# Six kept tiles around the middle layer boundary, and a transfer order in which each layer ends with its last wo block

## The chip, the cores and the metric

The kernel runs on one core of one Trainium2 chip. The metric is device time in microseconds (us), median of repeated runs. "Span" is the length of the one profiled execution; it is about 2 us shorter than the time of the same run.

Engine names as the profile has them: PE is the matmul engine (TensorE), PEld its weight loads, DVE is VectorE, ACT is ScalarE, POOL is GpSimd, SP is SyncE, which here only issues transfers ("SPq" is its queue). L425 is line 425 of the kernel profiled, so line numbers differ between kernels.

## The reference

One decode step of attention for one token, four layers deep. Layers 0 and 2 use the weights and the cache of set A, layers 1 and 3 those of set B. Each set holds K and V of 32 heads, 8192 positions, 192 columns, in bf16.

```python
def block(x, k_cache, v_cache, wq, wo):            # x: 1 x 640
    q = (x @ wq).reshape(32 heads, 192)
    scores = einsum("hd,hkd->hk", q, k) * 192 ** -0.5
    o = einsum("hk,hkd->hd", softmax(scores), v)
    return o.reshape(32 * 192) @ wo

x = x + block(layernorm(x), A_k, A_v, A_wq, A_wo)   # layer 0
x = x + block(layernorm(x), B_k, B_v, B_wq, B_wo)   # layer 1
x = x + block(layernorm(x), A_k, A_v, A_wq, A_wo)   # layer 2: the same cache as layer 0
x = x + block(layernorm(x), B_k, B_v, B_wq, B_wo)   # layer 3: the same cache as layer 1
```

K or V of one head is 8192 x 192 x 2 bytes = 3.146 MB, a "tile" below. Four layers of 64 tiles would be 256 tile loads. A tile that stays on the chip from layer 0 to 2, or from 1 to 3, saves one of them.

## The kernel before

SBUF holds eight slots of one tile each. All transfers go through these slots in one fixed list, `plan`, issued in order by SP; a transfer waits until the work that last read its slot is done. Five V tiles stay in their slot for two layers.

```python
NSLOT = 8
KEPT_A = (3, 9)          # V of these heads of set A stays from layer 0 to layer 2
KEPT_B = (18, 23, 28)    # V of these heads of set B stays from layer 1 to layer 3
...
for l in range(NL):
    for h in range(H):
        if h > 0 and h % HEADS_W == 0 and h <= H - O_LAST:     # before heads 10, 20, 30
            plan.append(("wo", l, h // HEADS_W - 1))           # 2.458 MB, into a slot
            steps.append(("wo", l, h // HEADS_W - 1))
        plan.append(("k", l, h))
        ...                       # m: K * q and its sums, s: softmax, v: p @ V
        plan += [n for n in part if n[0] == "v" and (l < 2 or n[2] not in kept[l % 2])]
        for g in {0: [0], 1: [1, 2]}.get(h, []):               # wq in three parts
            plan.append(("wq", l, g)); steps.append(("wq", l, g))
        if h == H // 2:
            plan.append(("wol", l))                            # last rows of wo, a tile of its own
...
# a slot for each transfer: the one whose holder is released first
i = min(range(NSLOT), key=lambda i: (-1 if holder[i] is None else released(holder[i]), i))
place[n], before[n] = i, holder[i]
```

For one head, DVE multiplies K by q in place in four pieces (L384), PE sums the products (S, L396), the softmax follows, and PE multiplies by V (O, L433). At the end of a layer the outputs of the last two heads are gathered and go through the last rows of wo ("YB" matmuls, L356), and the next layer's q can be computed only then.

Of the kernel before, what the change touches and what calls it, by code (L numbers as in the profile page):

```python
# [59 lines left out]
KEPT_A = (3, 9)  # L60
KEPT_B = (18, 23, 28)


def build(nc, A_x, A_k, A_v, A_wq, A_wo, B_x, B_k, B_v, B_wq, B_wo, out):
# [14 lines left out]
    G = 4  # L79

    with ExitStack() as ctx:
# [12 lines left out]
        wol = sb("wol", [P, OI, D], BF16)  # L94
        orow = sb("orow", [1, HEADS_W * DH], BF16)
        oT = sb("oT", [P, NW], BF16)
        o_sb = sb("o_sb", [P, 2 * DH], F32)
# [67 lines left out]
        kept = {0: KEPT_A, 1: KEPT_B}  # L165
        steps, plan = [], []
        for l in range(NL):
            if l == 0:
                plan.append(("wq0", 0))
            for h in range(H):  # L170
                if h > 0 and h % HEADS_W == 0 and h <= H - O_LAST:
                    plan.append(("wo", l, h // HEADS_W - 1))
                    steps.append(("wo", l, h // HEADS_W - 1))
                plan.append(("k", l, h))
                if h < H - 2:
                    part = [("m", l, h), ("s", l, h), ("v", l, h)]
                elif h == H - 2:
                    part = [("m", l, h)]
                else:
                    part = [("m", l, h), ("s", l, h - 1), ("s", l, h), ("v", l, h - 1), ("v", l, h)]  # L180
                steps += part
                plan += [n for n in part if n[0] == "v" and (l < 2 or n[2] not in kept[l % 2])]
                for g in {0: [0], 1: [1, 2]}.get(h, []):
                    plan.append(("wq", l, g))
                    steps.append(("wq", l, g))
                if h == H // 2:
                    plan.append(("wol", l))
                if h == H // 2 + 4 and l + 1 < NL:
                    plan.append(("wq0", l + 1))
        at = {n: i for i, n in enumerate(steps)}  # L190

        def released(n):

            if n[0] == "v" and n[1] < 2 and n[2] in kept[n[1]]:
                return at[("v", n[1] + 2, n[2])]
            return at[("m",) + n[1:] if n[0] == "k" else n]
# [12 lines left out]
        def transfer(n):  # L209
            l = n[1]  # L210
            w = W[l % 2]
            if n[0] == "wq0":
                return SP.op(lambda s: s.dma_start(
                    wq0[:], w["wq"][:, 0:Q_FIRST * DH].rearrange("(p c) n -> p c n", c=DC)),
                    freed.get(("wq0", l - 1)), sem=semQ0, inc=16)
            if n[0] == "wol":
                return SP.op(lambda s: s.dma_start(
                    wol[:], w["wo"][(H - O_LAST) * DH:H * DH].rearrange("(p i) n -> p i n", p=P)),
                    freed.get(("wol", l - 1)), sem=semOL, inc=16)
            i = place[n]  # L220
            t = slot[i]
            if n[0] in "kv":
                f = lambda s: s.dma_start(t[:], w[n[0]][0, n[2]].rearrange("(p j) d -> p (j d)", p=P))
            elif n[0] == "wq":
# [3 lines left out]
                    w["wq"][:, Q_FIRST * DH:].rearrange("(p c) n -> p c n", c=DC)[:, c0:c0 + k, :])  # L228
            else:
                r0 = n[2] * HEADS_W * DH  # L230
# [13 lines left out]
        def ahead():  # L244

            while issued[0] < len(plan):
# [4 lines left out]
                if m[0] in ("wq0", "wol") and m[1] > 0 and (m[0], m[1] - 1) not in freed:  # L251
                    return
# [7 lines left out]
        for k in "MX QB QT TT TO YB orow oT qT qbc xb rs st stt row_written".split():  # L260
            last[k] = None

        ev_x = SP.op(lambda s: s.dma_start(x_bf[:], A_x[0, 0].rearrange("(p c) -> p c", c=DC)), sem=semX, inc=16)
# [17 lines left out]
        def layer(l, ev_z, ev_true):  # L281
# [68 lines left out]
            def project(n, t3, k):  # L350

                PE.wait(last["oTw"], need(n), last["YB"])
# [213 lines left out]
```

## Time and profile before

2021.47 us, median of 3 runs (2019.82 to 2023.39); the profiled execution has a span of 2016.5 us.

From the page of the kernel before: busy time by engine; rows of the span in 40 slices of 50 us; the transfer totals and queues.

```profile
PE 1408.8 (70%) x10438; PEld 617.4 (31%) x10438; DVE 1047.1 (52%) x1073; ACT 217.1 (11%) x657; POOL 4.6 (0%) x22
GB/s 403 430 430 430 430 429 426 430 430 429 425 432 430 429 428 430 427 430 430 407 401 415 431 428 429 430 426 430 429 429 426 431 430 430 430 429 429 430 429 292
DMA packets 44211, 854.00 MB, mean 424 GB/s; under 512 B 4816, under 2 KB 7376, under 8 KB 7888
q1 hardware_dynamic: 44112, 852.51, 99.0%
q8 instruction: 82, 1.34, 0.3%
q14 instruction: 17, 0.14, 0.0%
```

No engine is near its limit, while the transfers run at 425 to 432 GB/s in nearly every slice. So the transfer stream is the bound, and a tile costs 3.146 MB / 430.5 GB/s = 7.3 us of it (430.5 is the plateau by the landings explained below: undisturbed tiles land 7.306 us apart). The stream is off this plateau at the start, around slices 20 to 22 (the boundary between layers 1 and 2), and at the end. q8 and q14 fetch the program's own instructions.

The end of the kernel, from its chain of waits (start us, length us, what; "x4" merges four instructions):

```profile
1949.65 41.19 DMA slot<-in_B_k_cache_dram
1990.87 6.78 DVE slot L384 x4
1997.69 1.47 PE S L396 x6
...
2003.10 2.35 PE O L433 x32
...
2007.55 2.69 PE O L433 x17
...
2012.37 0.78 PE YB L356 x15
```

The last K lands at 1990.9 us, 25.6 us of dependent work follow, and meanwhile the V tiles of the last two heads still arrive.

A transfer has landed when the last of the 16 DMA engines has raised its semaphore. I read each landing off the semaphore events in the trace. Three columns: the landing on the quickest engine, on the slowest, and how late it is (the gap to the previous landing on the slowest engine, less bytes / 430.5 GB/s). The trace does not name the engine of a landing, so "quickest" and "slowest" may be different engines from one transfer to the next. Kernel before, at the middle boundary:

```
transfer                quickest   slowest    late
K  layer 1, head 31      1004.9     1007.4     0.0
V  layer 1, head 31      1019.6     1022.0     0.0
K  layer 2, head 0       1026.9     1030.5     1.2
wq layer 2, part 0       1041.1     1044.7     0.0
K  layer 2, head 1       1052.7     1054.3     2.2
wq layer 2, part 2       1070.4     1072.4     0.5
K  layer 2, head 2       1078.4     1081.3     1.6
```

### The profile page before, as it was taken

How to read it: one execution, taken by the hardware profiler on the slowest of the kernel's cores; microseconds unless marked ns; L12 is line 12 of the kernel's file. 1: busy time of each engine (PE TensorE's matmuls, PEld its weight loads, DVE VectorE, ACT ScalarE, POOL GpSimd, SP SyncE). 2: the span in 40 equal slices, each digit the busy share in tenths (PEclk: the TensorE clock that was granted, in tenths of full speed). 3: DMA queues.
4: the chain of work that ended last, by engine and by line, in shares of the span. 5: the costliest groups of instructions: out<-in, count | busy, mean ns of one | idle time of the engine just before them, and what ended most of it. 6: DMA issues, size and time to landing. Idle time of an engine off the chain costs nothing.

```text
span 2016.5 us, 23357 instructions
## 1 busy us (share of the span) xinstructions
PE 1408.8 (70%) x10438; PEld 617.4 (31%) x10438; DVE 1047.1 (52%) x1073; ACT 217.1 (11%) x657; POOL 4.6 (0%) x22
## 2 busy tenths in 40 slices
PE   5667666667666766766766777667676667767777
PEld 2223223223332322322333233232233323223323
DVE  3455544555445455456544656546554454655554
ACT  0111111011011111111100111110100111011111
POOL 0000000000000000000000000000000000000000
PEclk8887988888777788788878978888877788888888
DMA  9999999999999999999999999999999999999996
GB/s 403 430 430 430 430 429 426 430 430 429 425 432 430 429 428 430 427 430 430 407 401 415 431 428 429 430 426 430 429 429 426 431 430 430 430 429 429 430 429 292
DMA packets 44211, 854.00 MB, mean 424 GB/s; under 512 B 4816, under 2 KB 7376, under 8 KB 7888
## 3 DMA queue, kind: packets, MB, share of 16 engines
q1 hardware_dynamic: 44112, 852.51, 99.0%
q8 instruction: 82, 1.34, 0.3%
q14 instruction: 17, 0.14, 0.0%
HBM read 852.49 MB, written 0.00 MB: 423 GB/s over the span
## 4 chain that ended last, share of the span: by engine, by line
DMA 68%; PE 17%; DVE 12%; ACT 1%; issue 1%; another core or an unknown queue 0%; SPq 0%; DVEq 0%
DMA slot<-in_B_k_cache_dram 34%; DMA slot<-in_A_k_cache_dram 31%; DVE slot L384 10%; PE S L396 10%; PE O L433 3%; DMA slot<-in_A_wq_dram 3%; PE TB L448 1%; DVE s_sb L403 1%; PE YB L356 1%; ACT p_sb L413 1%; PE TB L417 1%; DVE small L410 0%; PE QM L407 0%; DVE m_bf L406 0%
## 5 line engine op out<-in xcount | busy, mean ns | idle before, releaser
L384 DVE TENSOR_TENSOR slot<-slot,q_sb 128x3072 bf16<-128x3072 bf16 x512 | 865.7, 1753 | 492.1 <-DMA slot<-in_A_k_cache_dram 253.8
L396 PE MATMUL S<-slot,ident 128*128 128x512 bf16 x3072 | 849.4, 434 | 300.0 <-DVE slot L384 299.8
L396 PEld LDWEIGHTS S<-slot,ident 128*128 128x128 bf16 x3072 | 310.4, 109 | 834.6 <-DVE slot L384 442.4
L433 PE MATMUL O<-slot,p_sb 128*2 128x384 bf16 x4096 | 344.3, 417 | 0.0
L403 DVE TENSOR_REDUCE s_sb<-S 128x64 f32<-128x512 f32 x128 | 88.4, 690 | 251.0 <-PE S L396 251.0
L433 PEld LDWEIGHTS O<-slot,p_sb 128*2 128x2 bf16 x4096 | 128.0, 87 | 132.4 <-issue 96.1
L448 PE MATMUL TB<-o_sb,small 128*1 128x192 f32 x480 | 121.6, 386 | 36.5 <-DVE small L421 28.2
L346 ACT ACTIVATE q_sb<-QM 128x192 bf16<-128x192 f32 x120 | 39.6, 330 | 967.6 <-PE QM L339 967.6
L417 PE MATMUL TB<-small,ones 128*128 128x1 f32 x256 | 49.7, 263 | 109.6 <-ACT p_sb L413 109.6
L407 PE MATMUL QM<-ident,m_bf 128*128 128x128 bf16 x128 | 27.7, 217 | 130.8 <-DVE m_bf L406 130.8
L441 ACT ACTIVATE o_sb<-O,small 128x384 f32<-128x384 f32 x128 | 74.3, 580 | 227.2 <-PE O L433 227.2
L421 DVE RECIPROCAL small<-TB 128x1 f32<-128x1 f32 x128 | 21.6, 168 | 122.0 <-PE TB L417 122.0
L413 ACT ACTIVATE p_sb<-s_sb,small 128x64 bf16<-128x64 f32 x128 | 44.5, 348 | 337.5 <-DVE small L410 337.5
L417 PEld LDWEIGHTS TB<-small,ones 128*128 128x128 f32 x256 | 38.8, 191 | 129.4 <-ACT p_sb L413 129.4
L410 DVE TENSOR_REDUCE small<-QM 128x1 f32<-128x128 f32 x128 | 37.3, 291 | 52.3 <-PE QM L407 52.3
L454 ACT ACTIVATE orow<-TB 1x192 bf16<-1x192 f32 x120 | 38.3, 319 | 202.6 <-PE TB L448 202.6
L407 PEld LDWEIGHTS QM<-ident,m_bf 128*128 128x128 bf16 x128 | 12.2, 96 | 148.5 <-ACT q_sb L346 130.5
L448 PEld LDWEIGHTS TB<-o_sb,small 128*1 128x1 f32 x480 | 33.2, 88 | 76.3 <-DVE small L421 37.4
L356 PE MATMUL YB<-oT,slot 128*128 128x1 bf16 x900 | 37.9, 178 | 3.3 <-ACT oT L370 3.3
L356 PEld LDWEIGHTS YB<-oT,slot 128*128 128x128 bf16 x900 | 36.9, 131 | 4.3 <-ACT oT L370 4.3
L339 PEld LDWEIGHTS QM<-ident,qT 128*128 128x128 bf16 x240 | 22.9, 98 | 30.3 <-issue 2.0
L339 PE MATMUL QM<-ident,qT 128*128 128x128 bf16 x240 | 30.3, 209 | 1.6 <-ACT qT L328 1.6
(46 smaller groups left out, 189.3 us busy)
## 6 DMA issues: line engine op xcount, KB each, us to landing
slot<-in_A_k_cache_dram SPq DMA_DIRECT2D x64, 3072.0 KB, 31.6
slot<-in_B_k_cache_dram SPq DMA_DIRECT2D x64, 3072.0 KB, 31.4
slot<-in_A_v_cache_dram SPq DMA_DIRECT2D x62, 3072.0 KB, 32.0
slot<-in_B_v_cache_dram SPq DMA_DIRECT2D x61, 3072.0 KB, 30.5
slot<-in_A_wo_dram SPq DMA_DIRECT2D x6, 2400.0 KB, 30.1
slot<-in_B_wo_dram SPq DMA_DIRECT2D x6, 2400.0 KB, 30.9
slot<-in_A_wq_dram SPq DMA_DIRECT2D x4, 2880.0 KB, 21.2
slot<-in_B_wq_dram SPq DMA_DIRECT2D x4, 2880.0 KB, 31.3
```

The costliest lines, as they stand in the source:

```text
L339: e = PE.op(lambda t, b=b, o=o, n=n, d=done: t.matmul(QM[:, d:d + n], lhsT=qT[:, b:b + 1].broadcast_to([P, P]), rhs=ident[:, o:o + n], sta ...
L346: lambda a: a.activation(q_sb[i][:], QM[:, 0:DH], ACT.Copy), e, last["q"][i], bank=use["QM"])
L356: e = PE.op(lambda t, i=i, c=c, f=y_first[0], fin=fin: t.matmul(YB[:, c:c + 1], lhsT=t3[:, i, c:D:DC], rhs=oT[:, i:i + 1], start=f, stop=f ...
L384: e = DV.op(lambda v, d0=d0: v.tensor_tensor(k3[:, :, d0:d0 + QD], k3[:, :, d0:d0 + QD], q_sb[qi][:, d0:d0 + QD].unsqueeze(1).broadcast_to ...
L396: e = PE.op(lambda t, d0=d0, fin=fin: t.matmul(S[:, :], lhsT=ident[:], rhs=k3[:, :, d0:d0 + R], start=(d0 == 0), stop=fin), signal=fin, ba ...
L403: ev_s = DV.op(lambda v: v.tensor_reduce(s_sb[par][:], S[:].rearrange("p (j r) -> p j r", r=R), AX.X, ALU.add), ev_S[h], last["s"][par], b ...
L407: e = PE.op(lambda t: t.matmul(QM[:, C_MX:C_MX + P], lhsT=m_bf[par][:, 0:1].broadcast_to([P, P]), rhs=ident[:], start=True, stop=True), ev ...
L413: ev_p[h] = AC.op(lambda a: a.activation(p_sb[par][:], s_sb[par][:], ACT.Exp, bias=negm[par][:, 0:1], accum_out=l_col[par][:]), ev_n, ev_s ...
L417: e = PE.op(lambda t: t.matmul(TB[:, C_L + par:C_L + par + 1], lhsT=ones[:], rhs=l_col[par][:], start=True, stop=True), ev_p[h], last["L"] ...
L433: e = PE.op(lambda e, g=g, j=j, f=m < G, fin=fin: e.matmul(OB[par][32 * g:32 * g + 2, 0:2 * DH], lhsT=p_sb[par][:, j:j + 2], rhs=t[:, j * ...
L441: lambda a: a.activation(o_sb[:], OB[par][:, 0:2 * DH], ACT.Copy, scale=rl[par][:, 0:1]),
L448: e = PE.op(lambda t, i=i: t.matmul(TB[0:1, C_O:C_O + DH], lhsT=pick[:, i:i + 1], rhs=o_sb[:, i * DH:(i + 1) * DH], start=(i == 0), stop=( ...
```

## The change

Its intent is to load one tile less, to let the bulk of the last wo transfer run under the last heads' work, and to open layer 2 on tiles that are already there. K and V of head 0 of set A stay from layer 0 to 2, and V of heads 28 to 31 of set B from layer 1 to 3. Layer 3 takes its heads in another order, so that heads 30, 31 (first) and 28, 29 (places 8 and 9, counted from 0) meet their kept V early. In every layer the third wo block and the last wo rows now come after the last V and share one slot. A kept K cannot be multiplied in place, so head 0 of layer 0 writes its products into another slot ("t").

```diff
-KEPT_A = (3, 9)
-KEPT_B = (18, 23, 28)
+KEPT = {0: {("k", 0), ("v", 0)}, 1: {("v", 28), ("v", 29), ("v", 30), ("v", 31)}}
...
+    BACKWARD = dict(heads=[H - 2, H - 1] + list(range(H - HEADS_W, H - 2)) + list(range(O_LAST, H - HEADS_W))
+                    + list(range(O_LAST)), ...)
+    ORDER = [FORWARD, FORWARD, FORWARD, BACKWARD]
...
-        wol = sb("wol", [P, OI, D], BF16)
+        oTl = sb("oTl", [P, OI], BF16)
...
             if l == 0:
+                plan.append(("k", 0, 0))
                 plan.append(("wq0", 0))
+            wq_early = l == 2
+            if wq_early:
+                plan += [("wq", l, g) for g in range(len(Q_PARTS))]
...
+                if wq_early and p == 0:
+                    part = [("wq", l, 0), ("m", l, 0), ("wq", l, 1), ("s", l, 0), ("v", l, 0), ("wq", l, 2)]
...
-                if h == H // 2:
-                    plan.append(("wol", l))
...
+            plan.append(("wo", l, 2))
+            steps.append(("wo", l, 2))
+            plan.append(("wol", l))
...
-        ev_x = SP.op(lambda s: s.dma_start(x_bf[:], ...
+        ev_x = AC.op(lambda s: s.dma_start(x_bf[:], ...
...
+            if l + 1 == NL:      # the last add writes bf16 itself; no cast after it
+                return None, DV.op(lambda v: v.tensor_tensor(x_bf[:], x_true[:], YB[:, 0:DC], ALU.add), ...)
```

More of the change, by code (lines that the diff above doesn't have):

```diff
@@ L79, in build @@
     G = 4
+    FORWARD = dict(heads=list(range(H)), q0=0, q1=Q_FIRST * DH, wo=[0, HEADS_W, 2 * HEADS_W], wol=H - O_LAST)
+    BACKWARD = dict(heads=[H - 2, H - 1] + list(range(H - HEADS_W, H - 2)) + list(range(O_LAST, H - HEADS_W))
+                    + list(range(O_LAST)), q0=(H - Q_FIRST) * DH, q1=0,
+                    wo=[H - HEADS_W, O_LAST, O_LAST + HEADS_W], wol=0)
+    ORDER = [FORWARD, FORWARD, FORWARD, BACKWARD]
     with ExitStack() as ctx:
@@ L162, in build, with head, first_load, stays @@
             ev_zero = DV.op(lambda v, b=b: v.memset(b[:], 0.0), bank=use["O0" if b is OB[0] else "O1"])
-        kept = {0: KEPT_A, 1: KEPT_B}
+        def head(l, p):
+            return ORDER[l]["heads"][p]
+        def first_load(kind, l, p):
+            n = (kind, head(l, p))
+            if l >= 2 and n in KEPT[l - 2]:
+                return (kind, l - 2, ORDER[l - 2]["heads"].index(n[1]))
+            return (kind, l, p)
+        def stays(kind, l, p):
+            return l < 2 and (kind, head(l, p)) in KEPT[l]
         steps, plan = [], []
@@ L168, in build @@
             if l == 0:
+                plan.append(("k", 0, 0))
                 plan.append(("wq0", 0))
-            for h in range(H):
-                if h > 0 and h % HEADS_W == 0 and h <= H - O_LAST:
-                    plan.append(("wo", l, h // HEADS_W - 1))
-                    steps.append(("wo", l, h // HEADS_W - 1))
-                plan.append(("k", l, h))
-                if h < H - 2:
-                    part = [("m", l, h), ("s", l, h), ("v", l, h)]
-                elif h == H - 2:
-                    part = [("m", l, h)]
+            wq_early = l == 2
@@ new lines, in build @@
+            if wq_early:
+                plan += [("wq", l, g) for g in range(len(Q_PARTS))]
+            for p in range(H):
+                if p > 0 and p % HEADS_W == 0:
+                    b = p // HEADS_W - 1
+                    steps.append(("wc", l, b))
+                    if p <= H - HEADS_W:
+                        plan.append(("wo", l, b))
+                        steps.append(("wo", l, b))
+                if first_load("k", l, p) == ("k", l, p) and (l, p) != (0, 0):
+                    plan.append(("k", l, p))
+                if stays("k", l, p):
+                    plan.append(("t", l, p))
+                if wq_early and p == 0:
+                    part = [("wq", l, 0), ("m", l, 0), ("wq", l, 1), ("s", l, 0), ("v", l, 0), ("wq", l, 2)]
+                elif p < H - 2:
+                    part = [("m", l, p), ("s", l, p), ("v", l, p)]
+                elif p == H - 2:
+                    part = [("m", l, p)]
@@ L179, in build @@
                 else:
-                    part = [("m", l, h), ("s", l, h - 1), ("s", l, h), ("v", l, h - 1), ("v", l, h)]
+                    part = [("m", l, p), ("s", l, p - 1), ("s", l, p), ("v", l, p - 1), ("v", l, p)]
                 steps += part
-                plan += [n for n in part if n[0] == "v" and (l < 2 or n[2] not in kept[l % 2])]
-                for g in {0: [0], 1: [1, 2]}.get(h, []):
-                    plan.append(("wq", l, g))
-                    steps.append(("wq", l, g))
@@ L186, in build @@
-                if h == H // 2:
-                    plan.append(("wol", l))
-                if h == H // 2 + 4 and l + 1 < NL:
+                plan += [n for n in part if n[0] == "v" and first_load(*n) == n]
+                if not wq_early:
+                    for g in {0: [0], 1: [1, 2]}.get(p, []):
+                        plan.append(("wq", l, g))
+                        steps.append(("wq", l, g))
+                if p == H // 2 + 4 and l + 1 < NL:
                     plan.append(("wq0", l + 1))
+            plan.append(("wo", l, 2))
@@ L190, in build @@
+            steps.append(("wo", l, 2))
+            plan.append(("wol", l))
         at = {n: i for i, n in enumerate(steps)}
         def released(n):
-            if n[0] == "v" and n[1] < 2 and n[2] in kept[n[1]]:
-                return at[("v", n[1] + 2, n[2])]
-            return at[("m",) + n[1:] if n[0] == "k" else n]
+            if n[0] in "kvt":
+                l, p = n[1:]
+                if n[0] != "t" and stays(*n):
+                    l, p = n[1] + 2, ORDER[n[1] + 2]["heads"].index(head(*n[1:]))
+                return at[("v" if n[0] == "v" else "m", l, p)]
@@ L198, in build @@
+            return at[n]
         place, before, holder = {}, {}, [None] * NSLOT
@@ L210, in transfer @@
             l = n[1]
+            o = ORDER[l]
             w = W[l % 2]
@@ L213, in transfer @@
                 return SP.op(lambda s: s.dma_start(
-                    wq0[:], w["wq"][:, 0:Q_FIRST * DH].rearrange("(p c) n -> p c n", c=DC)),
+                    wq0[:], w["wq"][:, o["q0"]:o["q0"] + Q_FIRST * DH].rearrange("(p c) n -> p c n", c=DC)),
                     freed.get(("wq0", l - 1)), sem=semQ0, inc=16)
             if n[0] == "wol":
+                wol = slot[place[("wo", l, 2)]][:, NW * D:(NW + OI) * D].rearrange("p (i n) -> p i n", n=D)
                 return SP.op(lambda s: s.dma_start(
-                    wol[:], w["wo"][(H - O_LAST) * DH:H * DH].rearrange("(p i) n -> p i n", p=P)),
-                    freed.get(("wol", l - 1)), sem=semOL, inc=16)
+                    wol, w["wo"][o["wol"] * DH:(o["wol"] + O_LAST) * DH].rearrange("(p i) n -> p i n", p=P)),
+                    sem=semOL, inc=16)
             i = place[n]
             t = slot[i]
+            if n[0] == "t":
+                b = before[n]
+                return None if b is None else freed[b]
             if n[0] in "kv":
-                f = lambda s: s.dma_start(t[:], w[n[0]][0, n[2]].rearrange("(p j) d -> p (j d)", p=P))
+                f = lambda s: s.dma_start(t[:], w[n[0]][0, head(*n[1:])].rearrange("(p j) d -> p (j d)", p=P))
             elif n[0] == "wq":
@@ L227, in transfer @@
                     t[:, 0:k * QC].rearrange("p (c n) -> p c n", c=k),
-                    w["wq"][:, Q_FIRST * DH:].rearrange("(p c) n -> p c n", c=DC)[:, c0:c0 + k, :])
+                    w["wq"][:, o["q1"]:o["q1"] + QC].rearrange("(p c) n -> p c n", c=DC)[:, c0:c0 + k, :])
             else:
-                r0 = n[2] * HEADS_W * DH
+                r0 = o["wo"][n[2]] * DH
                 f = lambda s: s.dma_start(
@@ L250, in ahead @@
                     return
-                if m[0] in ("wq0", "wol") and m[1] > 0 and (m[0], m[1] - 1) not in freed:
+                if m[0] == "wq0" and m[1] > 0 and (m[0], m[1] - 1) not in freed:
                     return
@@ L259, in build @@
                     osb=None, orowb=None)
-        for k in "MX QB QT TT TO YB orow oT qT qbc xb rs st stt row_written".split():
+        for k in "MX QB QT TT TO YB orow oT oTl qT qbc xb rs st stt row_written".split():
             last[k] = None
-        ev_x = SP.op(lambda s: s.dma_start(x_bf[:], A_x[0, 0].rearrange("(p c) -> p c", c=DC)), sem=semX, inc=16)
+        ev_x = AC.op(lambda s: s.dma_start(x_bf[:], A_x[0, 0].rearrange("(p c) -> p c", c=DC)), sem=semX, inc=16)
         ahead()
@@ L348, in layer, with project @@
             y_first = [True]
-            def project(n, t3, k):
-                PE.wait(last["oTw"], need(n), last["YB"])
+            def project(n, t3, k, o, ev_o):
+                PE.wait(ev_o, need(n), last["YB"])
                 for i in range(k):
@@ L356, in project @@
                         e = PE.op(lambda t, i=i, c=c, f=y_first[0], fin=fin: t.matmul(
-                            YB[:, c:c + 1], lhsT=t3[:, i, c:D:DC], rhs=oT[:, i:i + 1], start=f, stop=fin,
+                            YB[:, c:c + 1], lhsT=t3[:, i, c:D:DC], rhs=o[:, i:i + 1], start=f, stop=fin,
                             skip_group_check=True), signal=(i == k - 1 and c == DC - 1), bank=use["YB"])
                         y_first[0] = False
-                last["oT"] = freed[n] = e
+                if n != ("wo", l, 2):
+                    freed[n] = e
                 return e
@@ L369, in columns @@
                 last["orow"] = e
-                last["TT"] = last["oTw"] = AC.op(lambda a: a.activation(oT[:, 0:k], TB[:, 0:k], ACT.Copy),
-                                                 e, last["oT"], bank=use["TB"])
+                last["TT"] = AC.op(lambda a: a.activation(oT[:, 0:k], TB[:, 0:k], ACT.Copy),
+                                   e, last["oT"], bank=use["TB"])
             ev_S, ev_p, ev_rl, ev_os = {}, {}, {}, {}
@@ L376, in products @@
                 par = (l * H + h) % 2
-                nk = ("k", l, h)
-                k3 = slot[place[nk]][:].rearrange("p (j d) -> p j d", d=DH)
+                nk = first_load("k", l, h)
+                nt = ("t", l, h) if stays("k", l, h) else nk
+                kin = slot[place[nk]][:].rearrange("p (j d) -> p j d", d=DH)
+                k3 = slot[place[nt]][:].rearrange("p (j d) -> p j d", d=DH)
                 qi = (l * H + h) % 3
-                DV.wait(need(nk), ev_q[h])
+                DV.wait(need(nk), need(nt), ev_q[h])
                 chunks = []
@@ L384, in products @@
                     e = DV.op(lambda v, d0=d0: v.tensor_tensor(
-                        k3[:, :, d0:d0 + QD], k3[:, :, d0:d0 + QD],
+                        k3[:, :, d0:d0 + QD], kin[:, :, d0:d0 + QD],
                         q_sb[qi][:, d0:d0 + QD].unsqueeze(1).broadcast_to([P, J, QD]), ALU.mult))
@@ L397, in products @@
                                                                      start=(d0 == 0), stop=fin), signal=fin, bank=use[f"S{par}"])
-                freed[nk] = ev_S[h] = e
+                freed[nt] = ev_S[h] = e
             def softmax(h):
@@ L425, in values @@
                 par = (l * H + h) % 2
-                a_keep = h in kept[l % 2]
-                nv_ = ("v", l - 2 if l >= 2 and a_keep else l, h)
+                nv_ = first_load("v", l, h)
                 t = slot[place[nv_]]
@@ L437, in values @@
                 last["p"][par] = e
-                if not (l < 2 and a_keep):
+                if not stays("v", l, h):
                     freed[nv_] = e
@@ L466, in gather_last @@
                 last["osb"] = e
-                last["TTn"] = last["oTw"] = AC.op(
-                    lambda a: a.activation(oT[r0:r0 + n, 0:OI], TB[r0:r0 + n, 0:OI], ACT.Copy), e, last["oT"], bank=use["TB"])
+                last["TTn"] = AC.op(
+                    lambda a: a.activation(oTl[r0:r0 + n, 0:OI], TB[r0:r0 + n, 0:OI], ACT.Copy), e, last["oTl"], bank=use["TB"])
             todo = None
@@ L489, in layer @@
                     q_ready = n[2] == len(Q_PARTS) - 1 or q_ready
-                else:
+                elif n[0] == "wc":
                     todo()
@@ L493, in layer @@
                     columns(NW)
-                    project(n, slot[place[n]][:, 0:NW * D].rearrange("p (i n) -> p i n", n=D), NW)
+                    last["oTw"] = last["TT"]
+                else:
+                    if todo is not None:
+                        todo()
+                        todo = None
+                    last["oT"] = project(n, slot[place[n]][:, 0:NW * D].rearrange("p (i n) -> p i n", n=D), NW, oT, last["oTw"])
                 following = [m[2] for m in here[i + 1:] if m[0] == "m" and m[2] not in ev_q][:1]
@@ L498, in layer @@
                 ahead()
-            todo()
             last["TT"] = last["TTn"]
-            ev_y = project(("wol", l), wol[:], OI)
+            wol = slot[place[("wo", l, 2)]][:, NW * D:(NW + OI) * D].rearrange("p (i n) -> p i n", n=D)
+            last["oTl"] = ev_y = freed[("wo", l, 2)] = project(("wol", l), wol, OI, oTl, last["TTn"])
+            if l + 1 == NL:
+                return None, DV.op(lambda v: v.tensor_tensor(x_bf[:], x_true[:], YB[:, 0:DC], ALU.add), ev_y, ev_true, bank=use["YB"])
             if l + 1 < NL:
@@ L509, in build @@
             ev_z, ev_true = layer(l, ev_z, ev_true)
-        e = DV.op(lambda v: v.tensor_copy(x_bf[:], x_true[:]), ev_true)
-        e = SP.op(lambda s: s.dma_start(out[0, 0].rearrange("(p c) -> p c", c=DC), x_bf[:]), e, sem=semOUT, inc=16)
+        e = SP.op(lambda s: s.dma_start(out[0, 0].rearrange("(p c) -> p c", c=DC), x_bf[:]), ev_true, sem=semOUT, inc=16)
         SP.wait(e)
```

## The prediction

> **What bounds the kernel.** The transfers. The page gives 854.00 MB at 424 GB/s over a 2016.5 us span; nearly every 50 us slice sits at 425 to 432 GB/s, PE is busy 70%, DVE 52%. The Trainium skill ("DMA: Bandwidth & Descriptors", Specifications) puts the fabric ceiling at 435 GB/s; the plateau of 430 agrees, so the rate cannot rise. Time comes only from fewer bytes, or from stretches off the plateau. A K or V tile (3.146 MB) takes 7.3 us of the stream.
>
> Off the plateau are three places. The start (403 in slice 1; first weights land at 5.0 us). The middle layer boundary (407, 401, 415), where three ring slots are left beside five kept tiles; by landing times, late transfers cost about 5 us there. The end: the last K lands at 1990.9 (chain of waits), the last V at 2005.4, the span ends at 2016.5: 25.6 us of work after the last K, 11.0 after the last byte.
>
> **What changes.**
> 1. Six tiles kept instead of five: 250 instead of 251 K/V loads, **-7.3 us** of stream.
> 2. The third wo block and last wo rows (2.95 MB, 6.85 us) now follow the last V. The last K lands 21.5 us before the stream ends instead of 14.6. Its tail gains the 75-matmul projection (3.2 us, timeline) that used to run before the last two heads, and loses a cast and an add (-0.4): 28.4 us after the last K, 6.9 after the last byte instead of 11.0: **-4.1 us**.
> 3. Middle boundary: layer 2 opens on kept K and V, wq loads first. With T0 = last K's landing, layer 1 ends at about T0+25.2 (3.2 later than before). wq part 1 reuses the wo slot and is issued then; before, a transfer issued to an almost drained queue landed 10.8 us after its release, for 7.3 us of data, so I count 3.5 us latency: part 1 is 0.4 us late. The first K load waits for head 0's matmuls (T0+38 to 39.5) while the stream drains at T0+39: 2 to 4 us late. Stall about 3.5 instead of 5: **-1.3 us**, my least certain term.
> 4. Start: first K issued ahead of x and wq; x moves to ACT: **-0.4 us**. The same page (Issuing engines are not separate DMA queues) says this saves only issue time.
> 5. Layer 2 runs on four ring slots throughout. Before had four for heads 3 to 9 at 430 GB/s, so no loss; other boundaries have slack. Head order costs nothing.
>
> Sum -13.1 us: **2008.4 us**, range 2003 to 2013. Faster by over 2%: 0.01; within 2%: 0.98; slower by over 2%: 0.01.
>
> **What would show it.** HBM read 849.3 MB (-3.15). V loads: A 63, B 60; K of A 63. Plateau 430 in layer 2's slices. Last K to end about 28.4 us, with the 75 matmuls on YB near the chain's end. Middle slices still dipping, with a DMA-queue wait on head 0's S matmuls early in layer 2.
>
> **What would make it wrong.** A middle boundary without stall (-3.5 more), or one much deeper with only two free slots (+5 to +8). Four slots failing over all of layer 2, visible as slices at 415 to 425: up to +10. Projection or wo landing later at the tail (+3). Instruction fetches (16 KB, about 1.1 us each on one DMA engine) falling differently: a few us either way.

## The result, and the profile after

2006.31 us, median of 4 runs (2005.45 to 2007.09), against 2020.64 us of the kernel before in the same rounds (2019.18 to 2023.39). The ratio is 0.9928, 95% interval 0.9914 to 0.9942. Ratios are the mean time of one kernel's runs over that of the other's of the same rounds, so not quite the ratio of the medians. In these rounds the kernel before scatters by some 4 us (later by 4.5 to 7), the changed one by less than 2.5.

The same rows of the page for the changed kernel:

```profile
PE 1402.4 (70%) x10438; PEld 616.8 (31%) x10438; DVE 1047.3 (52%) x1072; ACT 217.2 (11%) x657; POOL 4.6 (0%) x22
GB/s 404 431 430 430 429 430 426 430 431 429 425 431 429 431 429 430 426 431 430 429 361 431 430 430 430 431 426 429 429 430 426 430 428 428 431 430 431 430 430 325
DMA packets 44067, 850.85 MB, mean 424 GB/s; under 512 B 4800, under 2 KB 7360, under 8 KB 7872
q8 instruction: 82, 1.34, 0.3%
```

3.15 MB less are moved at the same plateau. Layer 2 (slices 21 to 30), now on four slots throughout, holds 426 to 431 after its first slice. The three middle dips have become one of 361.

The end, from the chain of waits of the changed kernel. The last K lands at 1976.0:

```profile
1976.05 6.78 DVE slot L425 x4
1982.88 1.47 PE S L437 x6
...
1988.56 2.69 PE O L473 x18
...
1993.34 2.69 PE O L473 x18
...
1998.13 3.71 PE YB L394 x90
```

From the last K to the end it is 28.9 us instead of 25.6: the 90 YB matmuls (75 + 15) now stand at the end. But the last byte lands at 1997.5, so only 7.5 us of the span have an idle stream, where it was 11.1.

The middle boundary. First the issues of SP in the timeline of the changed kernel (start, us, what; the time covers waits between merged issues):

```profile
1009.29 24.00 SPq L264 DMA_DIRECT2D slot<-in_A_wq_dram  x3
1040.90 0.34 SPq L261 DMA_DIRECT2D slot<-in_A_k_cache_dram  x1
```

Then, in the timeline of DVE, the products of heads 0 and 1 of layer 2, with the idle time before them and what ended it:

```profile
1028.77 6.76 DVE L425 TENSOR_TENSOR slot<-slot,q_sb 128x3072 bf16<-128x3072 bf16 x4 [1.95 <-ACT q_sb L344]
1051.65 6.77 DVE L425 TENSOR_TENSOR slot<-slot,q_sb 128x3072 bf16<-128x3072 bf16 x4 [7.03 <-DMA slot<-in_A_k_cache_dram]
```

K of head 1 is issued at 1040.9, when head 0's sums are done, as the prediction had it. Its landing, and the others':

```
transfer                quickest   slowest    late
K  layer 1, head 31       992.0     1000.6     0.0
wo, last wo rows         1013.6     1022.1     0.0
wq layer 2, part 0       1020.5     1030.3     1.3
wq layer 2, part 1       1033.7     1037.2     0.1
wq layer 2, part 2       1038.3     1041.2     0.6
K  layer 2, head 1       1050.1     1051.6     3.1
V  layer 2, head 1       1057.4     1059.0     0.0
```

Two things are to be seen. The quickest engines wait far longer than the slowest: between wo and wq part 1 the quickest gets 20.1 us for 13.7 us of data, the slowest 15.1. They had been 8 us ahead, and the boundary takes that lead away. The dip of 361 averages over all 16 engines; the time of the kernel is set by the last one. So a deeper dip in the GB/s row (lost over slices 20 to 22: 7.8 us before, 8.0 after, each slice's shortfall from 430 times 50 us) goes with a smaller loss on the slowest engine (summed lateness from K of layer 1's head 31 to head 5 of layer 2: 6.2 us before, 5.3 after). In each of these two sums one entry is no wait for a slot: wq part 0 after, K of head 0 before, each 1.2 to 1.3 us late on the slowest engine alone, with the quickest on time and the issue well ahead. They are steps of the kind treated under "More instructions"; without them the stall at the boundary is 5.0 us before and 4.0 after.

Where the 11.5 us of the two spans went, by the slowest engine's landings:

```
term                                       before    after    difference
bytes at 430.5 GB/s                        1980.2   1972.9     -7.3
late at the start (to V of head 0)            4.0      4.3     +0.3
late in layers 0 and 1                        8.5      8.3     -0.2
late at the middle boundary                   6.2      5.3     -0.9
late in the rest of layers 2 and 3            6.5      6.7     +0.2
last byte to the end                         11.1      7.5     -3.6
span                                       2016.5   2005.0    -11.5
```

The medians differ by 14.3 us, 3 more than the spans. I take that for scatter: the profiled execution of the kernel before (span 2016.5, so a time near 2018.6 if it is 2.1 us above the span as elsewhere) was faster than all four timed runs beside it, and that of the changed kernel was the slowest of its four (2007.09).

### The profile page after: what moved, and what is told of

It reads as the page before. It is cut to its first block, busy times and chain, and to the rows that moved or that the text cites. A ratio compares the mean times of both kernels' runs of the same rounds, so it can differ in the third digit from the quotient of the medians. Undisturbed runs are those within 1.5% of the kernel's fastest.

```text
span 2005.0 us, 23356 instructions
## 1 busy us (share of the span) xinstructions
PE 1402.4 (70%) x10438; PEld 616.8 (31%) x10438; DVE 1047.3 (52%) x1072; ACT 217.2 (11%) x657; POOL 4.6 (0%) x22
## 3 DMA queue, kind: packets, MB, share of 16 engines
q8 instruction: 82, 1.34, 0.3%
## 4 chain that ended last, share of the span: by engine, by line
DMA 67%; PE 19%; DVE 12%; ACT 1%; issue 1%; another core or an unknown queue 0%; POOL 0%; DVEq 0%; ACTq 0%
DMA slot<-in_A_k_cache_dram 33%; DMA slot<-in_B_k_cache_dram 32%; PE S L437 13%; DVE slot L425 10%; PE O L473 2%; DMA slot<-in_A_wq_dram 1%; PE TB L488 1%; DVE s_sb L444 1%; DMA x_bf<-in_A_x_dram 1%; ACT p_sb L454 1%; PE QT L358 1%; PE YB L394 1%; PE TB L458 0%; DVE small L451 0%
## 5 line engine op out<-in xcount | busy, mean ns | idle before, releaser
L437 PE MATMUL S<-slot,ident 128*128 128x512 bf16 x3072 | 839.5, 429 | 286.6 <-DVE slot L425 286.6
```

Source lines behind the costliest of these rows:

```text
L437: e = PE.op(lambda t, d0=d0, fin=fin: t.matmul(S[:, :], lhsT=ident[:], rhs=k3[:, :, d0:d0 + R], start=(d0 == 0), stop=fin), signal=fin, ba ...
```

## The experiments

My theory, A: three terms act on one stream, namely a tile less, a shorter idle stream at the end, and a slightly smaller stall at the middle; wherever a slot is freed 3.5 us or more before the queue drains, it costs nothing. Rival B: only bytes count, so the order of wo is idle. Rival C: the stall of the slowest engine at the middle is free, because the others catch it up or the gain is lost again later. Others are named where they come up. All edits are to the changed kernel. Times below are means of five runs; the changed kernel itself had means of 2006.29, 2005.78 and 2006.01 in three calls, and I use 2006.0 where its own run was not in the call. That comparison across calls is coarser than the scatter within one: the kernel before had means of 2020.1, 2018.1, 2019.3 and 2019.7 in the four calls, which ran on different chips. The call with 2018.1 is the one of the old wo order in layer 1, the old start, seven slots and more instructions; against the run with the old start in that call the other three are 0.3 us less slow than stated below.

### Yardsticks

No edit.

> The changed kernel once more, unedited, as the yardstick for the other three of this call. All theories: a ratio near 0.993 (0.991 to 0.995) to the kernel before, median about 2006 us, and a middle dip of the transfers of about 3.7 us as in its first profile.

2005.78 us, ratio 0.9929 (0.9916 to 0.9941). Its trace has a last-byte-to-end of 6.3 us instead of 7.5, which is the scatter of that term: in the first trace the 32 O matmuls of each of the last two heads took 2.73 us, at a granted clock of 0.50; here they took 2.10 (clock 0.66) and 2.73 (0.50).

> The changed kernel again, unedited, as the yardstick of this call: mean near 2006 us, 0.993 of the kernel before.

2006.01 us, ratio 0.9934. The yardstick repeats within 0.5 us.

### The last wo block before the last heads again, in layer 3

```diff
+EARLY_WO = (3,)
-                    if p <= H - HEADS_W:
+                    if p <= H - HEADS_W or l in EARLY_WO:
...
+                if p == H // 2 and l in EARLY_WO:
+                    plan.append(("wol", l))          # into a tile of its own, as before
```

(A scratch tile was cut from 48 to 36 columns to make room; only 36 are used.)

> The changed kernel, but in the last layer alone the third wo block is loaded and used before the last two heads again, and the last wo rows in mid-layer in a tile of their own. Theory A (my tail term): the last K then lands only 14.6 us before the last byte instead of 21.5, last byte to end goes from 7.5 us back to about 10.7, so 3 us slower than the changed kernel (2009). Rival B (the gain of the change is the missing tile and the middle; the place of wo does not matter because the bytes are the same): within 0.5 us of the changed kernel.

2010.88 us, 5.1 slower than the changed kernel of the same call. A holds and B falls; the size is 2 us more than I expected. The last byte lands at 1997.4, as in the changed kernel's first trace (1997.5), and the span ends 11.7 us after it. The chain of waits of this run at the end:

```profile
1982.87 6.78 DVE slot L430 x4
...
1995.31 2.69 PE O L478 x18
...
2000.09 2.69 PE O L478 x17
...
2005.15 0.78 PE YB L399 x15
```

The last K lands 6.8 us later than in the changed kernel, for 6.85 us of wo moved ahead of it, and no 75 matmuls stand at the end. So the end is worth 3.6 us by the two first traces and 5.1 by this pair of means. The term scatters: over the eleven traces that end in the new order (the reordered tail below aside) it is 5.8 to 7.7 us, over the two with the old order 11.1 and 11.7. PE's clock is one reason: with both O products in 1.47 us (granted clock 1.00, in the run with the old start) it is 5.8.

### Five kept tiles

```diff
-KEPT = {..., 1: {("v", 28), ("v", 29), ("v", 30), ("v", 31)}}
+KEPT = {..., 1: {("v", 29), ("v", 30), ("v", 31)}}
```

> The changed kernel with V of head 28 of the second set not kept but loaded again in the last layer: 251 tiles as in the kernel before, five ring slots in layer 2. Rival B (only bytes count): 7.3 us slower than the changed kernel (2013.6). Theory A: the extra slot at the middle boundary takes away the late transfers there (3.7 us in the trace of the changed kernel), so that only 3.5 us of the tile's 7.3 are lost: 2009 to 2010, with no dip at the middle boundary for the slowest engine.

2010.22 us, 4.4 slower. The tile costs its 7.3 us of stream, and the freed slot gives part back: K of head 1 now takes the slot of wq part 0 and lands 0.03 us late instead of 3.1; lateness at the middle is 1.7 us instead of 4.6 to 5.3, and 1.6 of that is the step at wq part 0, so hardly any stall is left. (In this trace the rest of layers 2 and 3 is 7.9 us late instead of 6.4 to 6.8, so not all of the gain need be kept.) So the sixth tile is worth 4.4 us, not 7.3, because it takes the slot the boundary needs. B, which wanted 7.3, falls. Compared with the kernel before, at the same 852.49 MB, this kernel is 9.9 us faster: that much comes from the order of the transfers and from which tiles are kept, not from their number.

### K of head 1 before the last part of wq

```diff
-                plan += [("wq", l, g) for g in range(len(Q_PARTS))]
+                plan += [("wq", l, 0), ("wq", l, 1), ("k", l, 1), ("wq", l, 2)]
...
-                if first_load("k", l, p) == ("k", l, p) and (l, p) != (0, 0):
+                if first_load("k", l, p) == ("k", l, p) and (l, p) not in ((0, 0), (2, 1)):
```

> The changed kernel with one swap of the transfer order at the start of layer 2: K of head 1 before the last part of wq, so that K takes the slot of wq part 0 (free at about T0+32 us) and the short wq part waits for head 0's K (free at T0+40) instead. Theory A: both releases then come before the queue drains, the stall of 3.1 + 0.6 us goes, 3 to 4 us faster than the changed kernel (2002 to 2003), landing gap of K of head 1 about 7.3 us instead of 10.4. Rival C (the stall only lets one lagging DMA engine catch up, and what is gained here is lost again later): less than 1 us faster.

2003.43 us, 2.35 faster; this version beats both kernels. From the timeline of SP, the two issues:

```profile
1032.72 0.34 SPq L261 DMA_DIRECT2D slot<-in_A_k_cache_dram  x1
1040.69 0.34 SPq L264 DMA_DIRECT2D slot<-in_A_wq_dram  x1
```

And from that of DVE, head 1's products:

```profile
1044.85 6.76 DVE L425 TENSOR_TENSOR slot<-slot,q_sb 128x3072 bf16<-128x3072 bf16 x4 [0.44 <-DMA slot<-in_A_k_cache_dram]
```

K of head 1 lands 0.5 us late instead of 3.1 (2.3 in the yardstick), and the short wq part 0.9 instead of 0.6 (0.3). Lateness at the middle falls from 4.6 to 2.7 us, and 0.7 of it comes back in the rest of layers 2 and 3, where it goes from 6.4 to 7.2. So A holds in its direction, the size is about two thirds of what I expected, and in this trace C takes a small share. Why the wq part is late although it was issued 4.1 us before the previous landing, I did not find out; by A's own rule of 3.5 us it should not have been. The spans of the two traces differ by only 1.3 us, because the yardstick's was its fastest execution.

> The swap of K of head 1 and the last part of wq again, to see whether its 2.35 us repeat against the changed kernel of the same call: 1.5 to 3 us faster (2003 to 2004.5). If it was a difference of the moment: within 1 us.

2003.67 us against 2006.01: 2.3 us again. The wq part is 1.5 us late this time. Here the later lateness was 6.7 against 6.8, so the share that I gave to C did not repeat.

### The old wo order in layer 1 alone

The edit of the run with the old order in layer 3, for the other layer:

```diff
-EARLY_WO = (3,)
+EARLY_WO = (1,)
```

> The changed kernel, but in layer 1 alone the third wo block and the last wo rows are loaded and used before the last two heads. Theory A (at the middle boundary the wo block fills the stream while the last heads of layer 1 are computed; without it the wq and first K loads of layer 2 wait): the late transfers grow from about 4 to about 7 us for the slowest engine, 3 us slower than the changed kernel (2009). Rival B (same bytes, same time): within 0.5 us.

2009.36 us, 3.3 slower than 2006.0 (3.0 slower than the start experiment below). K of head 1 of layer 2 is 5.9 us late and lateness at the middle is 7.8 us. A holds, B falls: the wo block after the last V is also what keeps the stream busy while layer 1's last heads are computed.

### The old start

```diff
-                plan.append(("k", 0, 0))
                 plan.append(("wq0", 0))
+                plan.append(("k", 0, 0))
...
-        ev_x = AC.op(lambda s: ...
+        ev_x = SP.op(lambda s: ...
```

> The changed kernel with the start of the kernel before: x first, then wq of the first heads, then the first K, all issued by SP. Theory A (the start is bound by the transfers, and the x load on ACT, though it lands at 11.5 us instead of 2.2 behind the first K, delays nothing that the stream waits for): within 1 us of the changed kernel (2005 to 2007), although head 0's products begin at 12.4 us again instead of 17.5. Rival D (the 5 us of later products at the start cost time, so the old start is the better one): 3 to 5 us faster. Rival E (the new start is worth the 0.4 us that I predicted, or more): 0.5 to 1 us slower.

2006.33 us, against 2006.0 no difference, but by the ratios to the kernel before (0.9941 here; 0.9928, 0.9929 and 0.9934 for the changed kernel, with intervals that overlap) the old start would be 1.4 to 2.6 us slower. Times alone do not settle half a microsecond; the traces say more. In the timeline, head 0's first products of the kernel before and of the changed one:

```profile
12.43 6.76 DVE L384 TENSOR_TENSOR slot<-slot,q_sb 128x3072 bf16<-128x3072 bf16 x4 [5.00 <-DMA slot<-in_A_k_cache_dram]
```

```profile
11.55 0.17 DVE L303 CAST small<-x_bf 128x5 f32<-128x5 bf16 x1 [9.60 <-DMA x_bf<-in_A_x_dram]
17.46 3.43 DVE L425 TENSOR_TENSOR slot<-slot,q_sb 128x3072 bf16<-128x3072 bf16 x2 [2.40 <-ACT q_sb L344]
```

The x load of 1.2 KB takes 10.8 us to land instead of 1.7, and head 0 starts 5 us later. It costs nothing that shows in the stream: 47.5 us of transfers (20.4 MB) were queued in free slots, and the lateness up to V of head 0 is 4.0 us with the old start, 4.0 to 4.3 with the new one. Nor does the earlier K gain anything: wq and K together are there at 12.7 instead of 12.4 us. The Trainium skill ("DMA: Bandwidth & Descriptors", Queues, rings and completion order) says that a DMA engine changes between queues only at packet boundaries, and takes the queues in turn. The trace agrees: x comes as 128 pieces of 10 bytes on a queue of its own, eight to an engine, and these start from 3.3 to 9.9 us, one about every 0.91 us on an engine, which is the time of one 24,576-byte packet of K. So x did not wait for K as a whole; each of its pieces waited for one packet of K. D (the late products cost time) falls. E's gain of half a microsecond or more is not seen in the stream, and the times can neither confirm nor exclude it.

### Seven slots

```diff
-NSLOT = 8
+NSLOT = 7
```

> The changed kernel with seven slots instead of eight, so three ring slots in layer 2 and one at the middle boundary. Theory A (four slots in layer 2 have some 6 us of slack, so three still just keep up with the stream; only the boundary, where wo, both wq parts and K of head 1 follow one another through one slot, stalls by about 15 us instead of 4): 11 to 15 us slower than the changed kernel (2017 to 2021), slices of layer 2 after the boundary still at 425 to 430 GB/s. Rival G (four slots are already at the edge in all of layer 2): 30 us slower or more, slices of layer 2 at 400 or less.

2017.40 us, 11.4 slower than 2006.0 (2014.82 to 2020.9, a wide scatter), at the lower edge of A. The GB/s row of its page:

```profile
GB/s 404 431 432 428 431 430 424 430 430 429 425 432 429 429 429 431 426 429 429 414 309 429 430 426 429 429 418 429 429 429 425 430 429 429 430 429 430 429 430 339
```

The loss is at the boundary: 14.1 us late there instead of 4.6 to 5.3, from wo, both big wq parts and K of head 1 following one another through one slot. After it, layer 2 runs on three slots at 425 to 430, with one slice of 418. So four slots through layer 2 are not at the edge, and G falls. What a slot is worth is decided at the boundary.

### More instructions

The lateness outside the boundary comes in steps on the slowest engine alone, about once every 200 us (in layers 0 and 1 of 1.1 to 1.7 us each, at V head 12 and K head 27 in layer 0, V heads 5 and 19 in layer 1, the same transfers in every variant but this run; in layers 2 and 3 they move). My prediction named instruction fetches as something that might fall differently. This run adds fetches and no data.

```diff
+            e_idle = ev_rs
+            for _ in range(1500):
+                e_idle = PO.op(lambda g: g.memset(idle[:], 0.0), e_idle)    # one column, never read
```

> The changed kernel with 6000 tiny memsets added on the idle POOL engine, 1500 after each layer's start, no data moved. Theory F (each 16 KB instruction fetch holds up one DMA engine for about 1.1 us; the steps of about 1.2 us by which landings fall behind every 200 us are these, and the slowest engine sets the time): the instruction queue grows from 82 packets to 105 or more, and with eight engines taking turns the kernel gets 3 to 6 us slower (2009 to 2012). Rival H (the steps have another cause; fetches are absorbed): no change within 1 us.

2019.94 us, 13.9 slower than 2006.0: F's direction, at more than twice my size. From the page:

```profile
PE 1412.9 (70%) x10438; PEld 619.2 (31%) x10438; DVE 1047.3 (52%) x1072; ACT 217.3 (11%) x657; POOL 594.1 (29%) x6022
DMA packets 44115, 851.24 MB, mean 422 GB/s; under 512 B 4801, under 2 KB 7361, under 8 KB 7873
q8 instruction: 82, 1.34, 0.3%
q14 instruction: 65, 0.52, 0.1%
```

I had named the wrong queue: q8 did not grow, q14 did, by 48 packets and 0.38 MB, which is 0.05% of all bytes. In the trace they come about every 20 us while the memsets run, and at the same pace landings slip by 0.65 us a step on one engine:

```
K of head 14, layer 0      quickest   slowest
changed kernel               239.3      242.8
more instructions            239.2      248.7
few long memsets (below)     239.6      242.7
```

The quickest engine notices nothing; the slowest falls behind, because nearly all of the added packets seem to go to the same engine: from 203.5 to 248.7 us the latest of the 16 landings falls from 8.1 to 9.5 us behind the quickest, while one other slips once by 1.5 us (a q8 packet) and the rest stay within 0.05. That is why my size was wrong: I had spread the fetches over eight engines, as the 82 packets in 2005 us against one step in 200 us had suggested. A q14 packet itself is recorded with 0.31 us, half of the slip; what the other half is stays open.

The rival is POOL's own work. The last run gives POOL more busy time and more bytes written, but few instructions:

```diff
+            for _ in range(100):
+                e_idle = PO.op(lambda g: g.memset(orow[64:P, :], 0.0), e_idle)    # 64 x 1920, rows never read
...
```

(The tile `orow` was given 128 partitions for this, and the next layer's POOL operation waits for the memsets.)

> The rival cause of the slow kernel with 6000 tiny memsets: not their fetches but POOL's own work and its SBUF writes. Here POOL gets as much busy time or more from 400 long memsets (64 partitions, 1920 elements), so far more bytes written but hardly any instructions. Theory F (the fetches do it): within 1.5 us of the changed kernel (2005 to 2007.5), two or three instruction packets more. Rival J (POOL's work slows the transfers or DVE): 10 us slower or more, as with the tiny memsets.

2006.40 us, as the changed kernel. Its page:

```profile
PE 1403.1 (70%) x10438; PEld 616.8 (31%) x10438; DVE 1047.2 (52%) x1072; ACT 217.6 (11%) x657; POOL 681.9 (34%) x422
q14 instruction: 20, 0.16, 0.0%
```

J falls. The fetches of the added instructions, not the work, made the kernel 13.9 us slower (0.38 MB for 6000 memsets is some 64 bytes an instruction; that each memset also waits on a semaphore was not separated, but the slips come at the pace of the packets, not of the memsets). The steps of the unedited kernels agree with q8's 82 packets of about 1.07 us each (they look like PE's: 2 x 10438 instructions of 64 bytes would be 1.34 MB, the queue's total). The changed kernel's trace supports this: between 60 and 320 us, 11 q8 packets start, and each time the 16 landing times of that transfer or the next slip by 1.4 to 1.7 us a packet, all 16 added up and beyond their even pace, on one engine as far as the sorted times show; two q14 packets go with 0.7 and 1.0, and elsewhere the sum stays under 0.35. No run removed a packet, so this is a coincidence in time, if a close one.

### Another order of the last three heads

On top of the swap of K of head 1 (the numbers below are places in layer 3's order, not head numbers):

```diff
+                elif l == NL - 1 and p >= H - 3:
+                    part = {H - 3: [("m", l, p)], H - 2: [("m", l, p), ("s", l, p - 1)],
+                            H - 1: [("m", l, p), ("v", l, p - 2), ("wc", l, 2), ("s", l, p - 1), ("s", l, p),
+                                    ("v", l, p - 1), ("v", l, p)]}[p]
```

("wc", which gathers the heads at places 20 to 29, moves with it.)

> On top of that swap, the last three heads of the last layer take their K loads one after the other (K29, K30, K31, then V29, V30, V31, wo), with the computing order changed to suit. If the end is bound by the work after the last K, which then lands 28.8 us before the last byte instead of 21.5, the end comes up to 1.5 us sooner after the last byte. If, as I count it, the work after the last V and the wo projection (about 5.9 us after the last byte) takes over at once, it gains 0.2 to 1 us: 2002.5 to 2003.5.

2004.40 us against 2003.67 of the swap: 0.7 slower, a miss. The last K does land early, at 1965.9, but then (chain of waits of this run):

```profile
1977.14 1.43 PE O L478 x32
1978.60 0.59 ACT o_sb L486
...
1980.45 1.06 PE TB L411 x15
...
1985.88 2.69 PE O L478 x18
1990.67 2.69 PE O L478 x32
```

The softmax of places 30 and 31 now stands in PE's order behind the V product, gather and columns of place 29, all of which used to be done earlier. What the load order gave, the computing order took: the O products of the last two heads start at 1985.8 us, in the swap's trace at 1985.7, although the last K landed 7.2 us earlier. From the last byte to the end it is 7.3 us in this trace and 6.3 in that of the swap; that difference is PE's speed, for the first of these products took 2.73 us here and 1.54 there. The O matmuls of one head take 1.43 us at one place of this chain and 2.69 at another. The Trainium skill ("TensorE: Matmul & The Clock Gate", Part 1) says that PE's clock is halved unless recent activity releases it. The halving is in this trace: the granted clock is 1.00 over the 1.43 us and 0.50 over both 2.69 us. No run here varies the activity on purpose.

## Why the prediction was right

2008.4 us (2003 to 2013) was forecast, 2006.31 measured.

- **The bound and the tile.** Right in mechanism and size as arithmetic on the stream: 3.15 MB less at the plateau of 430, 7.3 us. The plateau is just under the 435 GB/s that the Trainium skill ("DMA: Bandwidth & Descriptors", Specifications) gives as the ceiling. But the prediction treated the tile and the middle as separate terms. The run with five tiles shows that keeping the sixth is worth 4.4 us, as its slot would take about 3 us off the boundary's stall.
- **The end, -4.1.** Right: -3.6 between the two traces, 5.1 by undoing it. The last K to the end took 28.9 us (28.4 forecast), with the 75 matmuls next to the chain's end as forecast.
- **The middle, -1.3.** Right: -0.9 by lateness on the slowest engine (a stall of 5.0 before and 4.0 after, where the prediction had 5 and 3.5). The wait was the one named, K of head 1 on the sums of head 0, issued 40.3 us after the last K of layer 1 (38 to 39.5 forecast) and 3.1 us late (2 to 4 forecast). Reckoning latency from a drained queue in the trace of before, 3.5 us above the data's own time, was enough to place it; in the changed kernel that load took 10.7 us for 7.3 us of data.
- **The start, -0.4.** The one wrong term: the stream shows nothing of it (wq and K complete 0.3 us later; undoing it changed no lateness, and the times are too coarse for 0.4 us). I counted an earlier issue and overlooked that the first computation needs wq and x as well; x on ACT's queue landed 9 us later than before. "Saves only issue time" was read from the skill's page as a small gain at no risk; the trace shows no gain, and a delay of x that happened to be free. That it was free is luck: the prediction did not see it.
- **Four slots, head order: nothing.** Right for the slots: even three hold 425 to 430 GB/s in layer 2 but for one slice. The head order was not varied by itself; the lateness in the rest of layers 2 and 3 (6.5 before, 6.7 after) leaves no room for a large cost.
- **The sum.** -13.1 forecast, -11.5 between the spans, -14.3 between the medians; the two measurements differ, I take it, by which execution of the kernel before was profiled.

What stays open: the part of the swap's stall that did not turn into time, about 1 us; why the added q14 packets meet one engine; and what opening layer 2 on kept tiles is worth by itself. Of the 9.9 us by which the kernel with five tiles beats the kernel before, the wo order of layers 1 and 3 accounts for some 3.0 to 3.3 and 5.1 (measured with six tiles); the remainder was not taken apart.

## What to carry to other kernels

Where a transfer stream is the bound, cost a change by three things: bytes at the plateau, the time from the last byte to the end, and, for each slot reuse, whether its release comes early enough before the queue drains, with the latency of a drained queue taken from the trace. Put transfers that are needed last (here a weight block) behind the last data, so that they fill the stream while the dependent tail is computed, and remember that one more kept tile also takes a slot from the place where slots are scarce. Judge such a stream by its slowest DMA engine, not by the average rate: here a deeper dip in GB/s cost less, and 0.38 MB of extra instructions cost more (13.9 us) than a whole tile.

## What the Trainium skill lacked or had wrong

- "Runtime: NRT & Kernel Launch", Instruction fetch mechanics: fetches are called mostly hidden. Not in this transfer-bound kernel: 48 more packets on the q14 queue, 0.38 MB, made this one 13.9 us slower, with no change in DVE's busy time (1047.3 us), and the same POOL time from few instructions cost nothing. The page has refill blocks of 16 KiB; PE's queue agrees (82 packets, 1.34 MB), POOL's packets were of 8 KB.
- "DMA: Bandwidth & Descriptors": no section says that the gap between the 16 engines builds up over a steady stream. Here the slowest landed up to 9.8 us after the quickest (11.8 us with five kept tiles, 17.5 with more instructions), and at a stall the gap closes (8.6 us before the middle boundary, 1.6 after).
- The same page, Anatomy of one DMA, gives about 2.0 us of fixed cost for the gpsimd path only. For a 3.1 MB load issued by SP into a drained queue, the trace shows 1.9 us above the data's own time on the quickest engine and 3.4 on the slowest, which had 0.3 us of earlier work left.
- The same page, Issuing engines are not separate DMA queues: true here, but it does not warn what taking turns does to a tiny load in many pieces beside a large one: 10.8 us instead of 1.7 for 1.2 KB, each 10-byte piece behind a 24,576-byte packet.
